# Counting the chosen experts one step later, behind early blocks of the first two experts

## The chip, the cores and the metric

The kernel runs on one NeuronCore of a Trainium2 chip. Its engines are TensorE (PE, with a separate queue for weight loads, PEld), VectorE (DVE), ScalarE (ACT), GpSimd (POOL) and SyncE (SP, which here only issues DMAs). The metric is the device time of one execution in microseconds, as the median of several runs.

## What is computed

Three layers follow each other: causal attention with a decay, a dense feed-forward layer (2304 tokens, 512 wide, 2048 hidden), and a mixture of eight experts in which each token goes to the one expert with the largest gate.

```python
def _moe_ref(x, w_in, w_out):
    h = x @ w_in
    relu6 = np.clip(h + 3.0, 0.0, 6.0)
    g = h * relu6 / 6.0
    return (g @ w_out).astype(np.float32)

def _moe2_ref(x, w_gate, w_output_gate, w1, w2):
    logits = x @ w_gate
    e_idx = np.argmax(logits, axis=1)
    ...
    gate_w = probs[np.arange(N), e_idx]
    eom = 1.0 / (1.0 + np.exp(-(x @ w_output_gate)))
    for e in range(E):
        mask = e_idx == e
        ...
        h = np.maximum(x[mask] @ w1[e], 0.0)
        ye = h @ w2[e]
        out[mask] = gate_w[mask, None] * eom[mask, e, None] * ye
```

## The kernel before

**Numbers.** Every product is made of three matmuls of half-width parts (high times high, high times low, low times high), so each block of weights against a block of tokens costs three instructions. 

**The first two layers** share one long stretch: `moe1_steps` (L683) works on six chunks of 384 tokens, with L695 for the first weight and L718 for the second, and the attention (`attn_seq`, L557) is advanced between its steps. In this stretch a scheduler with a simulated timeline sets the order of every engine but SP, from priorities that follow the order of the code. A chunk of tokens, once it is out of the dense layer, goes through `gate_steps(c)` (L773), a generator: its first part multiplies with the gate weights (36 small matmuls, L783) and sends the rows through a DMA transpose (L791) to DRAM (`rows`, L793); the second part finds the best expert (L797 to L806), keeps a running count of the chosen experts over the 128-token tiles (`ohsum`, L809), multiplies it with a triangular matrix to get each token's rank in its expert (L814, L815), and makes the table entries `M` (L837). For the first five chunks the parts are run between steps 3, 5 and 7 of the next chunk.

**The seam.** After the last chunk nothing of the first two layers is left to interleave. The code there runs all of `gate_steps(5)`, then `count_rounds` (L886, one matmul L889 and the counts per expert, `cnt`). Then the order is written out by hand for PE, ACT and DVE (`manual_schedule`): two blocks of the first expert, `rank_onehot` for the last three tiles (L938), the `table` (L909: matmuls L916 and a chain of small DVE operations that ends in row numbers `ids`), and then the rest of the first products of experts 0 and 1 (`expert1`, L963, eight blocks of twelve matmuls each, L976, with L979 on ACT and L980 on DVE to empty each block's bank). These first products read 128 rows per expert that have been gathered earlier, from the first 15 tiles alone. They are followed by their second products (`expert2`, L984, L995).

**Behind the seam**, `round_` (L1160) gathers the other rows of every expert by index (L950 on POOL, an indirect DMA that needs `ids` and all of `rows`), transposes them (L953, a DMA that SP issues), multiplies them with both weights, and writes results out by index (L1002). The weights of experts 2 to 7 stream in meanwhile (`stw`, L866), and are split by ACT and DVE (L878, L879).

The blocks of the first two experts take their PSUM banks from the pool `ps_mm`, which has three; the pool `ps2` with five is opened only in front of `round_`:

```python
    first = [expert1(e, ps_mm, (0,)) for e in range(2)]
    ...
    ps2 = ctx.enter_context(tc.tile_pool(name="ps2", bufs=5, space=PSUM))
```

Of the kernel before, what the change touches and what calls it, by code (L numbers as in the profile page):

```python
# [15 lines left out]
PSUM = bass.MemoryType.PSUM  # L16
# [42 lines left out]
def attention_moe_kernel(ctx: ExitStack, tc: tile.TileContext, q, k, v, f, w_in, w_out,  # L59
# [5 lines left out]
    E, _, F2 = w1.shape  # L65
# [13 lines left out]
    ps_mm = ctx.enter_context(tc.tile_pool(name="ps_mm", bufs=3, space=PSUM))  # L79
# [693 lines left out]
    def gate_steps(c):  # L773
# [34 lines left out]
        for i in range(n):  # L808
            nc.vector.tensor_tensor(out=ohsum[:, f0 + i + 1], in0=ohsum[:, f0 + i], in1=oh[:, f0 + i],  # L809
                                    op=ALU.add)  # L810
        pr = ps_mm.tile([P, 512], F32, tag="mm", name="mm")
        for i in range(n):
            o = pr[:, i * E:(i + 1) * E]
# [72 lines left out]
    def count_rounds():  # L886

        ps = ps_mm.tile([P, 512], F32, tag="mm", name="mm")
        nc.tensor.matmul(ps[:, 0:E], lhsT=allone, rhs=ohsum[:, NB], start=True, stop=True)  # L889
        mx = mp2.tile([P, 1], F32, tag="cmx", name="cmx")  # L890
        more = mp2.tile([P, 8], F32, tag="more", name="more")
        nc.vector.tensor_reduce(out=mx, in_=ps[:, 0:E], axis=AX.X, op=ALU.max)
        nc.vector.tensor_tensor(out=more, in0=mx.to_broadcast([P, 8]), in1=thr, op=ALU.is_gt)
        nc.vector.tensor_reduce(out=mx, in_=more, axis=AX.X, op=ALU.add)
        nc.vector.tensor_copy(out=nrounds, in_=mx)
        nc.vector.tensor_copy(out=cnt, in_=ps[:, 0:E])
# [12 lines left out]
    def table(R, s0, pool, ps_pool, blocks, nb):  # L909


        n = len(blocks)
        sel = ps_pool.tile([P, 512], F32, tag="mm", name="mm")
        for j, s in enumerate(blocks):
            for i in range(nb):
                nc.tensor.matmul(sel[:, j * NV * E:(j + 1) * NV * E], lhsT=R[:, i, s * P - s0:(s + 1) * P - s0],  # L916
                                 rhs=M[:, i].rearrange("p a e -> p (a e)"), start=i == 0, stop=i == nb - 1)
        T = lambda nm, sh, dt: pool.tile(sh, dt, tag=f"{nm}{n}", name=nm)
        sv = T("sv", [P, n, NV, E], F32)
        nc.vector.tensor_copy(out=sv, in_=sel[:, 0:n * NV * E].rearrange("p (s a e) -> p s a e", a=NV, e=E))  # L920
        ids, u, cf = T("ids", [P, 2, n, E], U32), T("u", [P, n, E], F32), T("cf", [P, n, E], F32)
        nc.vector.scalar_tensor_tensor(out=u, in0=sv[:, :, 0], scalar=float(P), in1=sv[:, :, 1], op0=ALU.mult,
                                       op1=ALU.add)
        nc.vector.tensor_copy(out=ids[:, 0], in_=u)
        nc.vector.tensor_tensor(out=u, in0=u, in1=sv[:, :, 6], op=ALU.add)
        nc.vector.scalar_tensor_tensor(out=u, in0=sv[:, :, 2], scalar=-4096.0, in1=u, op0=ALU.mult, op1=ALU.add)
        nc.vector.tensor_scalar(out=ids[:, 1], in0=u, scalar1=4096.0, scalar2=None, op0=ALU.add)
        nc.vector.tensor_tensor(out=cf, in0=sv[:, :, 3], in1=sv[:, :, 4], op=ALU.add)
        nc.vector.tensor_tensor(out=cf, in0=cf, in1=sv[:, :, 5], op=ALU.add)
        for j, s in enumerate(blocks):  # L930
            slot[s] = (ids[:, 0, j], ids[:, 1, j], cf[:, j])
# [5 lines left out]
    def rank_onehot(R, i, s0, s1):  # L937
        nc.vector.tensor_scalar(out=R[:, i], in0=iota[:, s0:s1], scalar1=rank[:, i:i + 1], scalar2=None,  # L938
                                op0=ALU.is_equal)
# [23 lines left out]
    def expert1(e, ps_pool, blocks):  # L963

        W1, (xs, o) = wts[e, 0], xs_t[e, blocks[0]]
        hT, ho = h_t[e, blocks[0]]
        w = len(blocks) * P
        hs = slice(ho, ho + w)
        for m in range(F2 // P):
            ps = ps_pool.tile([P, 512], F32, tag="mm", name="mm")  # L970
            i = 0
            for j in range(KD):
                for a, b2 in ((0, 0), (0, 1), (1, 0)):
                    l = W1[:, a, j, m * P:(m + 1) * P]
                    r = xs[:, b2 * KD + j, o:o + w]
                    nc.tensor.matmul(ps[:, 0:w], lhsT=l.bitcast(BF16) if a else l, rhs=r.bitcast(BF16) if b2 else r,  # L976
                                     start=i == 0, stop=i == 3 * KD - 1)
                    i += 1
            nc.scalar.activation(out=hT[:, m, 0, hs], in_=ps[:, 0:w], func=AF.Relu)  # L979
            nc.vector.scalar_tensor_tensor(out=hT[:, m, 1, hs].bitcast(BF16), in0=ps[:, 0:w], scalar=0.0,  # L980
                                           in1=hT[:, m, 0, hs], op0=ALU.max, op1=ALU.subtract)
            yield
# [25 lines left out]
    def run(g, n=1):  # L1008

        last = None  # L1010
        for _ in range(n):
            r = next(g, "end")
            last = r or last
            if r == "end":
                break
        return last
# [46 lines left out]
    gq = []  # L1063
# [12 lines left out]
    for c in range(NCH):  # L1076
# [55 lines left out]
        if c < NCH - 1:  # L1132
            while len(complete) < need[c + 1]:
                adv()
        gq.append(gate_steps(c))
    for g_ in gq:
        for _ in g_:
            pass
    run(wg_, 4 * KD + 1 - nw)
    count_rounds()  # L1140
    ET = mybir.EngineType

    first = [expert1(e, ps_mm, (0,)) for e in range(2)]
    manual = ctx.enter_context(ExitStack())
    manual.enter_context(tc.manual_schedule(engines={ET.PE, ET.Activation, ET.DVE}))
    run(first[0], 2)
    for i in range(NBL, NB):
        rank_onehot(R, i, P, CAP)
    table(R, P, const, ps_mm, (1, 2), NB)
    for g_ in first:  # L1150
        run(g_, F2 // P)
# [2 lines left out]
            pass  # L1154
    moe1_ctx.close()
    xp = ctx.enter_context(tc.tile_pool(name="xp", bufs=1))
    ps2 = ctx.enter_context(tc.tile_pool(name="ps2", bufs=5, space=PSUM))
    regs = []

    def round_(first):  # L1160
# [85 lines left out]
```

## Time and profile before

| | us |
|---|---|
| median of 3 runs | 831.59 (827.8 to 831.8) |
| the profiled execution | 830.41 |
| its span, from the first to the last instruction | 828.7 |
| the stretch of attention and dense layer with gates in it | about 190 to 588 |
| the seam | about 588 to 619 |
| the experts' rounds | 619 to the end |

The rows below come from the profiled execution. Times count from its first instruction. "Idle before" is the time for which the engine had nothing to run, with the instruction that ended it behind the arrow.

### The profile page before, as it was taken

The page shows a single profiled execution, that of the slowest core. Times are in us where ns is not written, and L with a number is a line of the kernel's source. Part 1 is how long each engine was busy: PE and PEld are TensorE (multiplying, and loading weights), DVE is VectorE, ACT ScalarE, POOL GpSimd, SP SyncE. Part 2 cuts the span into 40 slices and gives each one's busy share as a digit, 9 for nine tenths or more (in the row PEclk, how much of TensorE's full clock was granted, in tenths as well). Part 3 has the DMA queues.
Part 4 walks back from the last instruction along what each step waited for, and adds up shares of the span by engine and source line. Part 5 has one row for each costly group of instructions (what it writes and reads, how often), then busy time and mean ns, then how long its engine had stood idle before and what let it go on. Part 6 is the DMA issues. An engine that isn't in the chain of part 4 may idle for free.

```text
span 828.7 us, 16710 instructions
## 1 busy us (share of the span) xinstructions
PE 744.0 (90%) x6177; PEld 478.4 (58%) x6177; DVE 470.3 (57%) x1267; ACT 449.9 (54%) x909; POOL 317.2 (38%) x393
## 2 busy tenths in 40 slices
PE   4745989978899999998999999999899999999993
PEld 2533556645655655565665666566668665667641
DVE  7998988547651865158623776760313555554510
ACT  4864789756882775277724654550113545454510
POOL 9546788845753463145522500000131232310010
PEclk9986989989999999998999999999999999999997
DMA  8758799979985783497623847612474899895410
GB/s 248 214 184 192 180 214 257 193 128 167 176 154 116 138 141 74 74 145 143 107 55 67 145 138 238 177 41 51 78 150 94 240 281 267 231 265 200 149 37 29
DMA packets 263778, 127.95 MB, mean 154 GB/s; under 512 B 214658, under 2 KB 247522, under 8 KB 263684
## 3 DMA queue, kind: packets, MB, share of 16 engines
q1 hardware_dynamic: 251860, 105.20, 58.5%
q0 software_dynamic: 4960, 15.73, 5.5%
q10 hardware_dynamic: 6864, 5.80, 2.6%
q8 instruction: 54, 0.88, 0.4%
q14 instruction: 40, 0.33, 0.1%
HBM read 71.52 MB, written 10.08 MB: 98 GB/s over the span
## 4 chain that ended last, share of the span: by engine, by line
PE 38%; DMA 28%; DVE 11%; issue 7%; ACT 7%; POOL 4%; SPq 2%; ACTq 0%; another core or an unknown queue 0%; POOLq 0%; DVEq 0%
PE mm L718 14%; PE mm L695 12%; DMA out_dram<-y,ids 7%; DMA stw<-in_moe_w_dram 4%; DMA xg<-rows,ids 4%; PE mm L976 4%; DMA pt<-pn 3%; PE mm L995 3%; PE sc L295 2%; DMA q<-qp 2%; DMA K<-kp 2%; DVE W L879 1%; ACT ms L376 1%; DMA ldk<-in_k_dram 1%; DVE g L707 1%
## 5 line engine op out<-in xcount | busy, mean ns | idle before, releaser
L695 PE MATMUL mm<-xT,wi 128*128 128x384 f16 (+1 forms) x1152 | 213.3, 335 | 7.5 <-DMA xT<-xn 5.1
L718 PE MATMUL mm<-g,wo 128*128 128x384 f16 (+1 forms) x1152 | 199.8, 326 | 1.9 <-ACT g L703 1.1
L695 PEld LDWEIGHTS <-wi 128*128 128x128 f16 (+1 forms) x1152 | 112.1, 100 | 85.2 <-issue 19.7
L718 PEld LDWEIGHTS <-wo 128*128 128x128 f16 (+1 forms) x1152 | 110.7, 98 | 75.2 <-issue 4.6
L976 PEld LDWEIGHTS <-W 128*128 128x128 f16 (+1 forms) x1344 | 100.6, 99 | 16.2 <-issue 8.0
L879 DVE TENSOR_TENSOR W<-stw,W 128x1024 bf16<-128x1024 f32 x64 | 77.7, 1224 | 52.8 <-ACT W L878 48.8
L376 ACT ACTIVATE ms<-ms,nm 128x512 f32<-128x512 f32 (+4 forms) x144 | 78.8, 576 | 48.5 <-DVE nm L342 27.1
L394 POOL TENSOR_TENSOR pn<-ms,pn 128x384 bf16<-128x384 f32 (+1 forms) x80 | 82.4, 1034 | 57.8 <-ACT pn L393 52.6
L976 PE MATMUL mm<-xs,W 128*128 128x256 f16 (+3 forms) x1152 | 97.1, 246 | 4.7 <-DVE hT L980 2.3
L995 PE MATMUL mm<-W,hT 128*128 128x512 f16 (+1 forms) x432 | 94.4, 379 | 1.0 <-DVE hT L980 0.6
L878 ACT ACTIVATE W<-stw 128x1024 f16<-128x1024 f32 x64 | 66.9, 1054 | 47.7 <-DMA stw<-in_moe_w_dram 45.4
L707 DVE TENSOR_TENSOR g<-hr,g 128x384 bf16<-128x384 f32 x80 | 58.1, 726 | 33.6 <-ACT g L703 33.4
L342 DVE CUSTOM_DVE_ANT_1 ms<-sc,mask 128x128 f32<-128x128 f32 (+3 forms) x128 | 59.2, 486 | 26.1 <-PE sc L295 12.1
L995 PEld LDWEIGHTS <-hT 128*128 128x128 f16 (+1 forms) x432 | 41.9, 98 | 51.3 <-issue 1.9
L702 DVE SCALAR_TENSOR_TENSOR hr<-hr,mm 128x384 f32<-128x384 f32 x96 | 52.7, 549 | 28.1 <-ACT hr L699 27.5
L703 ACT ACTIVATE g<-hr 128x384 f16<-128x384 f32 x96 | 49.4, 515 | 28.0 <-DVE hr L702 27.4
L699 ACT ACTIVATE hr<-mm,bias 128x384 f32<-128x384 f32 x96 | 54.4, 567 | 16.5 <-PE mm L695 14.5
L980 DVE SCALAR_TENSOR_TENSOR hT<-mm,hT 128x128 bf16<-128x128 f32 (+1 forms) x96 | 32.0, 355 | 50.4 <-ACT hT L979 48.1
L428 PE MATMUL pv<-vt,pt 128*128 128x65 f16 x320 | 41.2, 198 | 20.9 <-DVE xs L453 9.4
L1002 POOL DMA_INDIRECT out_dram<-y,ids x18 | 20.7, 1148 | 97.9 <-ACT y L1001 57.2
L295 PE MATMUL sc<-K,q 128*128 128x256 f16 (+3 forms) x192 | 48.7, 296 | 6.4 <-DVE nm L342 4.3
L393 ACT ACTIVATE pn<-ms 128x384 f16<-128x384 f32 (+1 forms) x80 | 44.3, 556 | 13.3 <-DMA pt<-pn 12.9
(189 smaller groups left out, 1113.5 us busy)
## 6 DMA issues: line engine op xcount, KB each, us to landing
stw<-in_moe_w_dram SPq DMA_DIRECT2D x64, 512.0 KB
wo<-in_moe_w_in_dram SPq DMA_DIRECT2D x16, 512.0 KB
raw<-in_moe_w_out_dram ACTq DMA_DIRECT2D x11, 512.0 KB
rows<-rw POOLq DMA_DIRECT2D x15, 256.0 KB, 3.5
ldk<-in_k_dram SPq DMA_DIRECT2D x14, 256.0 KB
ldq<-in_q_dram SPq DMA_DIRECT2D x14, 256.0 KB
ldv<-in_v_dram SPq DMA_DIRECT2D x13, 256.0 KB
g<-in_moe_w_out_dram SPq DMA_DIRECT2D x3, 512.0 KB
```

The source lines that it names most:

```text
L295: nc.tensor.matmul(po, lhsT=lhs[0:rows], rhs=r if n > 1 else r[:, :, 0], start=x == 0, stop=x == 1)
L342: nc.vector.tensor_tensor_reduce(out=pairs(ms[:, off:off + w]), in0=ps[:, 0:w].rearrange("p (c j) -> p c j", c=2), in1=pairs(mask[:, 640 - ...
L376: nc.scalar.activation(out=ms[:, off:off + w], in_=ms[:, off:off + w], func=AF.Exp, scale=-1.0, bias=nm[:, i:i + 1])
L394: nc.gpsimd.tensor_tensor(out=lo.bitcast(BF16), in0=ms[:, 0:N], in1=hi, op=ALU.subtract)
L695: nc.tensor.matmul(ps[:, 0:w], lhsT=l.bitcast(BF16) if a else l, rhs=r.bitcast(BF16) if b2 else r, start=i == 0, stop=i == 3 * KD - 1)
L699: nc.scalar.activation(out=hr, in_=ps[:, 0:w], func=AF.Relu, bias=bias3)
L707: either.tensor_tensor(out=g[:, m, 1, 0:w].bitcast(BF16), in0=hr, in1=g[:, m, 0, 0:w], op=ALU.subtract)
L718: nc.tensor.matmul(ps[:, 0:w], lhsT=l.bitcast(BF16) if a else l, rhs=r.bitcast(BF16) if b2 else r, start=i == 0, stop=i == 3 * NF - 1)
L878: nc.scalar.activation(out=hi, in_=sts[i], func=AF.Copy)
L879: nc.vector.tensor_tensor(out=lo.bitcast(BF16), in0=sts[i], in1=hi, op=ALU.subtract)
L976: nc.tensor.matmul(ps[:, 0:w], lhsT=l.bitcast(BF16) if a else l, rhs=r.bitcast(BF16) if b2 else r, start=i == 0, stop=i == 3 * KD - 1)
L995: nc.tensor.matmul(ps, lhsT=l.bitcast(BF16) if a else l, rhs=r.bitcast(BF16) if b2 else r, start=i == 0, stop=i == 3 * NF2 - 1)
```

## The change

`gate_steps` gets one more `yield`, between the running count `ohsum` and the rank matmuls. At the seam the last chunk's gate is no longer run as a whole: two blocks of expert 0 are issued first, then the gate's first two parts, three more blocks, the gate's rest with `count_rounds` and `rank_onehot`, the last three blocks of expert 0 and the first two of expert 1, then the table, and the other six blocks. `ps2` is opened ahead of this and gives the blocks their banks.

```diff
         for i in range(n):
             nc.vector.tensor_tensor(out=ohsum[:, f0 + i + 1], in0=ohsum[:, f0 + i], in1=oh[:, f0 + i],
                                     op=ALU.add)
+        yield
         pr = ps_mm.tile([P, 512], F32, tag="mm", name="mm")
...
-    for g_ in gq:
-        for _ in g_:
-            pass
     run(wg_, 4 * KD + 1 - nw)
-    count_rounds()
     ET = mybir.EngineType
-
-    first = [expert1(e, ps_mm, (0,)) for e in range(2)]
+    ps2 = ctx.enter_context(tc.tile_pool(name="ps2", bufs=5, space=PSUM))
+
+    first = [expert1(e, ps2, (0,)) for e in range(2)]
     manual = ctx.enter_context(ExitStack())
     manual.enter_context(tc.manual_schedule(engines={ET.PE, ET.Activation, ET.DVE}))
+    last, = gq
     run(first[0], 2)
+    run(last, 2)
+    run(first[0], 3)
+    run(last, 2)
+    count_rounds()
     for i in range(NBL, NB):
         rank_onehot(R, i, P, CAP)
+    run(first[0], 3)
+    run(first[1], 2)
     table(R, P, const, ps_mm, (1, 2), NB)
...
-    ps2 = ctx.enter_context(tc.tile_pool(name="ps2", bufs=5, space=PSUM))
```

The lines from L811 on have a number one higher in the new code.

On PE at the seam, before, the rank matmuls (L814, L815) stand right behind the gate's (L783):

```order
L783 LDWEIGHTS x_7847
L783 MATMUL mm<-wg,x_7847 128x16
L814 LDWEIGHTS tri
L814 MATMUL mm<-oh,tri 128x8
L815 LDWEIGHTS allone
L815 MATMUL mm<-ohsum,allone 128x8
```

On PE at the same place with the change, blocks of expert 0 (L977, before L976) stand ahead of them:

```order
L977 LDWEIGHTS W_7129
L977 MATMUL mm<-wi,W_7129 128x128
L815 LDWEIGHTS tri
L815 MATMUL mm<-oh,tri 128x8
L816 LDWEIGHTS allone
L816 MATMUL mm<-ohsum,allone 128x8
```

In all, PE's order at the seam was 36 gate matmuls, 6 for the rank, 1 for the count, 24 of expert 0, 36 of the table, then 168 of experts 0 and 1; it is now 24 of expert 0, 36 gate, 36 of expert 0, 6 rank, 1 count, 60 of experts 0 and 1, 36 table, 72 of expert 1.

On DVE at the seam, before, the gate's second part (up to L836 and M, L837) is mixed with the count (L894, L895) and has two blocks' emptying (L980) in it; L938 are the last tiles' ranks against a ruler:

```order
L894 TENSOR_REDUCE cmx<-more 128x1
L831 CAST vb<-z 128x3
L895 CAST nrounds<-cmx 128x1
L832 CAST vals<-vb 128x3
L833 TENSOR_TENSOR z<-z,vb 128x3
L980 SCALAR_TENSOR_TENSOR wi<-mm,wi 128x128
L834 CAST vb<-z 128x3
L835 CAST vals<-vb 128x3
L836 TENSOR_TENSOR vals<-z,vb 128x3
L980 SCALAR_TENSOR_TENSOR wi<-mm,wi 128x128
L938 TENSOR_SCALAR R<-iota,rank 128x256 x2
L837 TENSOR_TENSOR M<-vals,oh 128x168
```

On DVE with the change, at the end of that stretch, the count (L893 to L897) and the ruler (L939) stand behind M (L838), and five blocks' emptying (L981) stands between them and the table's chain, which begins with L921:

```order
L837 TENSOR_TENSOR vals<-z,vb 128x3
L838 TENSOR_TENSOR M<-vals,oh 128x168
L893 TENSOR_REDUCE cmx<-mm 128x1
L894 TENSOR_TENSOR more<-cmx,thr 128x8
L895 TENSOR_REDUCE cmx<-more 128x1
L896 CAST nrounds<-cmx 128x1
L897 CAST cnt<-mm 128x8
L939 TENSOR_SCALAR R<-iota,rank 128x256 x3
L981 SCALAR_TENSOR_TENSOR wi<-mm,wi 128x128 x5
L921 COPY sv<-mm 128x112
L923 SCALAR_TENSOR_TENSOR u<-sv 128x16
L925 CAST ids<-u 128x16
```

The count moved from inside the gate's chain to behind it, and the blocks' emptying from inside it to behind the ruler. SP's order of transposes and loads behind the seam stays as it was; on POOL one of seven gathers now stands behind the first write of results instead of ahead of it.

The new `yield` also moves the second half of the gates of the first five chunks, since each call now runs a shorter part (the rest falls to step 7 instead of 5), and with it the scheduler's choices from the first gate on. On DVE near the third gate, before, the gate's operations (L804, L805, L809) follow the attention's L469 at once; L707 is the dense layer's:

```order
L707 TENSOR_TENSOR g<-hr,g 128x384
L469 TENSOR_SCALAR xs<-pv,rl 64x64 x2
L804 TENSOR_REDUCE cm<-t_5169 128x3
L805 TENSOR_TENSOR oh<-t_5169,cm 128x24
L809 TENSOR_TENSOR ohsum<-ohsum,oh 128x8
L816 TENSOR_TENSOR t_5171<-lg,oh 128x24
```

On DVE near the third gate with the change, operations of the attention's scores (L342) have come in between, and L816 is L817:

```order
L707 TENSOR_TENSOR g<-hr,g 128x384
L469 TENSOR_SCALAR xs<-pv,rl 64x64 x2
L804 TENSOR_REDUCE cm<-t_5169 128x3
L805 TENSOR_TENSOR oh<-t_5169,cm 128x24
L342 ISA ms,nm<-sc,mask 128x2x64
L342 ISA nm 128x1
L342 ISA ms,nm<-sc,mask 128x2x128
L342 ISA nm 128x1
L809 TENSOR_TENSOR ohsum<-ohsum,oh 128x8
L817 TENSOR_TENSOR t_5171<-lg,oh 128x24
```

The pair L707 and L469 stayed together; what follows them changed places.

## Rows read from the trace of the kernel before

**Rows 1.** Windows by stage: length, busy us (count) by engine, granted clock, DMA share, GB/s.

```profile
core 0: us, PE busy (x) PEld busy (x) DVE busy (x) ACT busy (x) POOL busy (x), PEclk, DMA share, GB/s
190.00:588.00 398.00, 382.88 (x3071) 236.26 (x3068) 220.38 (x675) 221.59 (x451) 135.35 (x169) 0.99 0.61 121
588.00:619.00 31.00, 26.47 (x324) 19.77 (x322) 10.47 (x59) 5.82 (x20) 8.39 (x10) 0.94 0.71 137
643.00:815.00 172.00, 168.15 (x1202) 108.65 (x1199) 79.26 (x114) 80.06 (x130) 34.21 (x29) 1.00 0.68 203
```

**Rows 2.** Timeline of PE at the seam: start, length, line, count, idle before.

```profile
588.33 0.37 PE L783 MATMUL mm<-wg,x 128*128 128x16 f16 x9
589.08 0.21 PE L783 MATMUL mm<-wg,x 128*128 128x16 f16 x2 [0.37 <-ACT x L727]
589.67 0.79 PE L783 MATMUL mm<-wg,x 128*128 128x16 f16 x25 [0.39 <-DVE x L728]
591.84 0.18 PE L814 MATMUL mm<-oh,tri 128*128 128x8 f16 x1 [1.38 <-DVE oh L805]
...
592.53 2.72 PE L976 MATMUL mm<-wi,W 128*128 128x128 f16 x24
595.04 0.77 PE L916 MATMUL mm<-M,R 128*128 128x56 bf16 x15
596.57 0.86 PE L916 MATMUL mm<-M,R 128*128 128x56 bf16 x21 [0.77 <-DVE M L837]
597.28 5.57 PE L976 MATMUL mm<-wi,W 128*128 128x128 f16 x96
603.07 0.83 PE L976 MATMUL mm<-wi,W 128*128 128x128 f16 x12 [0.22 <-DVE wi L980]
605.26 3.51 PE L976 MATMUL mm<-wi,W 128*128 128x128 f16 x60 [1.36 <-DVE wi L980]
608.61 10.52 PE L995 MATMUL mm<-W,wi 128*128 128x512 f16 x48
618.97 3.51 PE L976 MATMUL mm<-xs,W 128*128 128x128 f16 x60
```

**Rows 3.** Windows of three pieces of the seam, columns as in the first group.

```profile
588.00:592.00 4.00, 1.86 (x43) 1.44 (x41) 1.96 (x12) 0.71 (x2) 0.00 (x0) 1.00 0.74 36
592.00:595.50 3.50, 3.46 (x41) 3.21 (x39) 2.27 (x21) 0.69 (x3) 0.59 (x1) 0.51 0.77 153
595.50:599.00 3.50, 2.73 (x62) 2.61 (x60) 2.44 (x13) 0.53 (x3) 1.11 (x2) 1.00 0.80 260
```

**Rows 4.** Timeline of DVE at the seam.

```profile
590.50 0.21 DVE L797 COPY lg<-mm 128x48 f32<-128x48 f32 x1 [0.88 <-PE mm L783]
...
592.21 0.16 DVE L809 TENSOR_TENSOR ohsum<-ohsum,oh 128x8 f16<-128x8 f16 x1
592.43 0.18 DVE L822 TENSOR_TENSOR t<-mm,oh 128x24 f32<-128x24 f32 x1
...
596.44 0.28 DVE L938 TENSOR_SCALAR R<-iota,rank 128x256 f16<-128x256 f16 x1
...
598.62 0.17 DVE L927 TENSOR_SCALAR ids<-u 128x16 uint32<-128x16 f32 x1
```

**Rows 5.** Timeline of POOL behind the seam.

```profile
600.32 0.99 POOL L950 DMA_INDIRECT xg<-rows,ids  x1 [2.70 <-PE mm L976]
...
609.21 0.94 POOL L950 DMA_INDIRECT xg<-rows,ids  x1 [5.37 <-DMA xs<-xg]
612.36 0.94 POOL L950 DMA_INDIRECT xg<-rows,ids  x1 [2.21 <-DMA xs<-xg]
```

**Rows 6.** Line 1194 on SP's queue, the reading of the counts.

```profile
L1194 SPq TENSOR_LOAD <-cnt x8: 262/388/1098, 594.9 to 600.5; - x8
```

**Rows 7.** PE's longest wait from 190 to 588 us, and line 707 (ns: min/median/max).

```profile
PE pv L428 <- DVE xs L469: 4.7, 1, 4.7
L707 DVE TENSOR_TENSOR g<-hr,g x80: 537/559/4343, 183.4 to 558.5; 128x384 bf16<-128x384 f32 x80
```

## Prediction

> **What bounds the kernel now.** I first read the windows by stage [rows 1]. From 190 to 588 us PE is busy 382.9 of 398 us, and from 643 to 815 us 168.2 of 172: there the time is PE's, and nothing off its path counts. In the 31 us of the seam it is busy only 26.5, at a mean clock of 0.94. So the seam is where this change can earn, and what it earns is read as one number: when PE starts the first matmul on newly gathered rows, 618.97 us [rows 2].
>
> The timeline of PE [rows 2] shows what the 30.64 us from 588.33 to there are made of. The gate's matmuls wait twice (0.37 and 0.39 us) for the last columns of x2 to be emptied by ACT and DVE. Then PE waits 1.38 us for DVE to find the chosen expert. 24 matmuls of expert 0 follow in 2.51 us (592.53 to 595.04), the table waits 0.77 us for M, and the other 168 matmuls take 11.33 us (597.28 to 608.61) with two waits (0.22 and 1.36 us) behind DVE's emptying of banks. A steady run of the same matmuls is the last 60: 605.26 to 608.61, or 0.0558 us each. At that rate the 24 would take 1.34 us; they are slow because the granted clock fell to 0.51 from 592.0 to 595.5 us, after a stretch in which PE was busy 1.86 of 4 us [rows 3].
>
> **The change, part by part.**
>
> *PE's order at the seam.* I lay the same instructions along the new order, each at its rate from [rows 2], from 588.33 us on.
> - 24 of expert 0, which need nothing from x2: 24 x 0.0558 = 1.34, to 589.67. That is when x2's last columns were ready before, so both short waits are covered.
> - 36 gate matmuls: the three pieces were busy 0.37 + 0.21 + 0.79 = 1.37 us, with their overlapping ends counted thrice; 1.2, to 590.9.
> - 36 of expert 0: 2.01, to 592.9. Meanwhile DVE finds the expert. From the copy of the logits to the last running count it needed 590.50 to 592.37 us [rows 4], 1.9 us; its start moves from 590.50 to about 590.9, and fewer operations are mixed in, so the count is there by 592.8 and the 1.38 us wait is covered, just.
> - 7 small matmuls for rank and count: 592.53 - 591.84 = 0.69 before, with waits in it. Bounds 0.2 and 0.7, I take 0.3: 593.2.
> - 60 of experts 0 and 1: 3.35, to 596.5.
> - The table's first 15, which need only old tiles: about 0.5, to 597.0. The other 21 need the ruler. 36 in all.
> - 21 of the table: 597.28 - 596.57 = 0.71. Then 72 of expert 1: 4.02. Then L995, 608.61 to 618.97 = 10.36.
>
> *DVE's chain* decides the gap in front of the 21. The gate's second part (16 operations), the count (5) and the ruler (3) now start when the emptying of block 4 is done, some 0.6 us behind PE's 592.9, at 593.5. From L797 to L822 fourteen operations took 590.50 to 592.43 [rows 4], 0.14 us each; 24 of them are 3.3 us and end at 596.8. If each waits its full length of about 0.2 us for the one before, they take 4.8 and end at 598.3. I take 597.4, nearer to the first since half of them are independent: PE waits 0.4 us, with bounds of 0 and 1.3.
>
> *The banks.* Between the emptying of block 4 and the end of the ruler DVE empties nothing, and exactly five blocks are issued by PE in that time. With the three banks of `ps_mm` PE would stand still for two of the five; with the five of `ps2` it does not. The cost of that edit alone is nothing, and its cover is the number five. The waits of 0.22 and 1.36 us sit behind ACT and DVE at 603 to 605 us. I don't know what held ACT there. With five banks PE can run two blocks, 1.3 us, further ahead, so most of the 1.58 us goes; bounds 0 and 1.6 left, I take 0.4.
>
> *Sum.* 597.0 + 0.4 + 0.71 + 4.02 + 10.36 + 0.4 = 612.9 against 618.97: 6.1 us earlier. The bounds add to 5 us (late ruler, waits stay in part) and 6.7 us (neither).
>
> *Does PE get its rows by 612.9?* The gather of the first rows started at 600.32 us [rows 5]. The fourth gather, at 609.21, had waited for the buffer that the first transpose frees, so the first rows were transposed by then, and the second rows by 612.36. That is ahead of 612.9 and, for the second, of 612.9 + 96 x 0.0558 = 618.3. In the new order `ids` comes later: the ruler at 597.4, then the 21 matmuls, five banks to empty, and the chain, near 599.9 instead of 598.8 [rows 4]. The first gather also needed the last rows in DRAM, which don't move; POOL stood idle until 600.32, 1.5 us after `ids` was done. So it moves by 0 to 1 us, and the slack of 3.7 us (612.9 - 609.2) covers that. SP reads the counts in front of the transposes, 594.9 to about 600.8 [rows 6]; the counts now come about 2 us later, so SP is free at about 603, still ahead of the landing of the gather.
>
> *Behind the seam* everything waits for PE: the transposes for expert 2 need a buffer that expert 0's product frees, and the splitting of its weights stands behind expert 1's blocks on ACT and DVE. From 643 us PE is idle 3.9 of 172 us [rows 1], so there is no store of waiting that would swallow the gain, and the 6.1 us reach the end.
>
> *The long stretch before.* The new `yield` moves the second half of five gates, and the scheduler has reshuffled every engine from about 198 us on. The matmuls are the same, so what can change is waiting: 15.1 us in this stretch [rows 1]. The largest piece is one wait of 4.7 us behind DVE's L469, which stood behind an L707 that took 4.34 us instead of the typical 0.56 [rows 7]. L707 and L469 are neighbours again in the new order. Bounds by this row: one such wait less (-4.7) or one or two more (+4.7, +9.4). Nothing in the rows says which; I take 0.
>
> The profiled execution took 830.41 us, and 830.41 - 6.1 = 824.3. The median of the runs is 1.2 above it, which gives 825.5; I predict 825.0.
>
> **Rivals.**
>
> *The clock falls all the same.* It fell from 1.00 to 0.51 behind a stretch with 1.86 of 4 us busy [rows 3]. In the new order PE has work in that stretch, but 36 of its matmuls are 16 columns wide, and the table waits again. If the same 3.5 us run at half rate, 1.7 us are lost: 612.9 becomes 614.6, and the time 826.7. The granted clock in the windows from 589 to 598 decides. [...]
>
> *The rows come too late.* If the gather starts more than about 3.7 us later (counts, `ids` or SP's reads each late), PE waits for rows instead. At 3 us beyond the slack the gain halves: 827.5. Against it stand the slacks above.
>
> *The stretch before gets better.* If the 4.7 us wait is gone, 825.0 - 4.7 = 820.3. For it: the change moves the very operations around L469. Against it: L707 and L469 still stand together.
>
> *The stretch before gets worse: slower.* The mechanism is an L707 stretched to 4.34 us with attention work behind it on DVE, and PE waiting 4.7 us for that. One more is 829.7, no measurable change; from two on the kernel is slower than the profiled 830.41: 834.4. It happened once among 80 in the old order [rows 7], so two more would be a changed pattern, but five gates are moved. [...]
>
> *The change does nothing at the seam*, since PE waits for the rows whatever it does ahead of them, cannot be: the second rows were ready 6.6 us before PE came for the first.
>
> **How the numbers follow.** Half a per cent (4.2 us) is about what a measurement of this kernel can tell from no change; faster means below 827.4. My chances: seam gain in full with the stretch before within 2 us, 0.45; the clock falls, 0.12; rows late, 0.07; stretch better by about 4.7, 0.16; worse by one such wait, 0.14; by two or more, 0.06. Faster takes in the first, the better stretch and most of the clock case: 0.68. Same takes in the late rows, one more wait and the rest: 0.26. Slower is 0.06. The range goes from below the better stretch, 819, to above one more wait, 831, and leaves out the slower case and the tails of the others. The likeliest case alone would be 823 to 827.
>
> **What the new profile would show.** PE goes from its last L718 to L977 without a gap; rank matmuls start within 0.3 us of the third block's end; the clock is 1.00 from 589 to 598; a gap of at most 1.3 us stands in the table; L996 begins at 602 to 603 us of the old time scale, and the first matmul on gathered rows at 612 to 614. The stretch from 190 to 588 us ends within 2 us of the old time. I am wrong if the last L718 moves by more than 4 us, if PE waits for transposed rows behind L996, or if the later rounds give the gain back in waits for weights.

## The result, and the profile after

The changed kernel took 820.85 us (median of 7 runs, 817.04 to 828.27) against 831.18 of the kernel before in the same runs (7, 827.8 to 831.8): ratio 0.9884, interval 0.9857 to 0.9911. That is 10 us faster, inside the predicted range of 819 to 831 and 4 us below the predicted 825.0. It lies nearer to the 820.3 of the rival with a better stretch, which had set the lower end of that range.

The profiled execution of these runs was the longest of the seven (828.27 us), so I read a second one of the same code beside it, called **again** below (813.19 us, its shortest). The first group shows the windows of the long stretch and of the seam of the first one, columns as in [rows 1]:

```profile
190.00:592.80 402.80, 386.54 (x3151) 239.66 (x3148) 218.61 (x686) 226.26 (x460) 138.79 (x174) 1.00 0.60 121
592.80:617.60 24.80, 23.89 (x321) 17.70 (x320) 10.74 (x59) 6.27 (x21) 6.51 (x8) 1.00 0.58 136
```

The seam now fits into 24.8 us, PE is busy in 23.9 of them, and the clock is 1.00 throughout (0.94 in [rows 1]). PE's timeline of again answers to [rows 2]; start, length, line, count, idle before:

```profile
580.01 1.50 PE L977 MATMUL mm<-wi,W 128*128 128x128 f16 x24
581.35 1.05 PE L783 MATMUL mm<-wg,x 128*128 128x16 f16 x36
582.25 2.17 PE L977 MATMUL mm<-wi,W 128*128 128x128 f16 x36
584.26 0.17 PE L815 MATMUL mm<-oh,tri 128*128 128x8 f16 x1
...
584.44 3.51 PE L977 MATMUL mm<-wi,W 128*128 128x128 f16 x60
587.79 0.55 PE L917 MATMUL mm<-M,R 128*128 128x56 bf16 x15
588.61 1.06 PE L917 MATMUL mm<-M,R 128*128 128x56 bf16 x21 [0.27 <-DVE R L939]
589.50 4.18 PE L977 MATMUL mm<-wi,W 128*128 128x128 f16 x72
593.52 10.52 PE L996 MATMUL mm<-W,wi 128*128 128x512 f16 x47
604.30 3.58 PE L977 MATMUL mm<-xs,W 128*128 128x128 f16 x60 [0.26 <-issue]
608.64 3.57 PE L977 MATMUL mm<-xs,W 128*128 128x128 f16 x61 [0.76 <-DVE hT L981]
```

From the first early block to the first gathered row it is 604.30 - 580.01 = 24.29 us (24.66 in the first profile), where [rows 2] have 30.64. All waits of [rows 2] are gone but one of 0.27 us in the table. A small one at 604.30 is new; the one behind `hT` at 608.64 had 0.52 us in the kernel before. The clock, in windows that answer to [rows 3]:

```profile
579.00:583.00 4.00, 4.00 (x82) 3.58 (x80) 1.54 (x6) 1.04 (x3) 0.00 (x0) 1.00 0.14 30
583.00:586.50 3.50, 3.50 (x70) 3.50 (x68) 3.14 (x21) 1.48 (x7) 0.94 (x2) 1.00 1.00 194
586.50:590.00 3.50, 3.23 (x72) 2.92 (x69) 3.26 (x21) 0.83 (x3) 0.26 (x2) 1.00 0.44 156
```

DVE's chain (answering to [rows 4]), the last write of rows and the first gather on POOL ([rows 5]) and the reading of the counts by three engines ([rows 6]), all of again:

```profile
582.44 0.21 DVE L797 COPY lg<-mm 128x48 f32<-128x48 f32 x1 [0.29 <-PE mm L783]
...
584.98 0.17 DVE L817 TENSOR_TENSOR t<-lg,oh 128x24 f32<-128x24 f32 x1
...
588.20 0.16 DVE L897 CAST cnt<-mm 128x8 int32<-128x8 f32 x1
588.27 0.67 DVE L939 TENSOR_SCALAR R<-iota,rank 128x256 f16<-128x256 f16 x3
...
590.36 0.17 DVE L925 CAST ids<-u 128x16 uint32<-128x16 f32 x1
```

```profile
589.97 0.54 POOL L793 DMA_DIRECT2D rows<-wi  x1 [3.24 <-DMA wi<-x]
593.21 0.99 POOL L951 DMA_INDIRECT xg<-rows,ids  x1 [2.70 <-PE mm L977]
```

```profile
L1198 SPq TENSOR_LOAD <-cnt x8: 262/264/524, 588.4 to 592.9; - x8
...
L1198 PEldq TENSOR_LOAD <-cnt x8: 300/312/927, 600.0 to 604.0; - x8
L1198 ACTq TENSOR_LOAD <-cnt x8: 274/384/708, 604.1 to 607.3; - x8
```

In the long stretch the 4.34 us L707 and the 4.7 us wait of [rows 7] are gone. Line 707 (ns: min/median/max), and PE's longest waits from 353.44 to 436.89 us, the part where the 4.7 us stood (in total, times, longest), again:

```profile
L707 DVE TENSOR_TENSOR g<-hr,g x80: 527/558/1939, 182.4 to 550.2; 128x384 bf16<-128x384 f32 x80
```

```profile
PE mm L695 <- DVE hr L702: 1.7, 1, 1.7
PE mm L815 <- DVE hr L702: 1.2, 1, 1.2
PE mm L718 <- DVE hr L702: 1.1, 1, 1.1
```

### The profile page after: what moved, and what is told of

The parts are those of the page before. It is cut to its first block, busy times and chain, and to the rows that moved or that the text cites. A ratio compares the mean times of both kernels' runs of the same rounds, so it can differ in the third digit from the quotient of the medians.

```text
span 826.5 us, 16712 instructions
## 1 busy us (share of the span) xinstructions
PE 741.9 (90%) x6166; PEld 478.6 (58%) x6177; DVE 466.5 (56%) x1267; ACT 450.2 (54%) x909; POOL 318.0 (38%) x393
## 4 chain that ended last, share of the span: by engine, by line
PE 41%; DMA 28%; DVE 11%; issue 7%; ACT 7%; POOL 4%; SPq 1%; ACTq 0%; POOLq 0%; DVEq 0%
PE mm L718 19%; PE mm L695 10%; DMA out_dram<-y,ids 8%; DMA pt<-pn 5%; DMA xg<-rows,ids 4%; PE mm L977 4%; PE mm L996 2%; DMA stw<-in_moe_w_dram 2%; DMA q<-qp 2%; DMA K<-kp 2%; PE sc L295 2%; DVE ms L342 2%; POOL pn L394 1%; ACT ms L376 1%; DVE cv L658 1%
## 5 line engine op out<-in xcount | busy, mean ns | idle before, releaser
L718 PE MATMUL mm<-g,wo 128*128 128x384 f16 (+1 forms) x1152 | 200.0, 328 | 1.7 <-DVE hr L702 1.7
L718 PEld LDWEIGHTS <-wo 128*128 128x128 f16 (+1 forms) x1152 | 111.5, 98 | 75.9 <-issue 5.4
L977 PEld LDWEIGHTS <-W 128*128 128x128 f16 (+1 forms) x1344 | 99.5, 98 | 15.0 <-issue 7.7
L977 PE MATMUL mm<-xs,W 128*128 128x256 f16 (+3 forms) x1152 | 97.0, 246 | 5.2 <-DVE hT L981 3.0
L996 PE MATMUL mm<-W,hT 128*128 128x512 f16 (+1 forms) x422 | 93.8, 379 | 1.1
L342 DVE CUSTOM_DVE_ANT_1 ms<-sc,mask 128x128 f32<-128x128 f32 (+3 forms) x128 | 59.0, 484 | 27.3 <-PE sc L295 13.5
L707 DVE TENSOR_TENSOR g<-hr,g 128x384 bf16<-128x384 f32 x80 | 54.1, 678 | 33.3 <-ACT g L703 33.1
L996 PEld LDWEIGHTS <-hT 128*128 128x128 f16 (+1 forms) x432 | 41.8, 98 | 51.0 <-issue 1.6
L703 ACT ACTIVATE g<-hr 128x384 f16<-128x384 f32 x96 | 49.3, 516 | 24.1 <-DVE hr L702 23.5
L981 DVE SCALAR_TENSOR_TENSOR hT<-mm,hT 128x128 bf16<-128x128 f32 (+1 forms) x96 | 31.6, 353 | 49.9 <-ACT hT L980 49.4
L428 PE MATMUL pv<-vt,pt 128*128 128x65 f16 x320 | 42.0, 198 | 17.9 <-DVE xs L453 10.8
L728 DVE SCALAR_TENSOR_TENSOR x<-mm,x 128x384 bf16<-128x384 f32 x24 | 13.2, 555 | 71.7 <-ACT x L727 71.7
```

What stands on the lines that cost most here:

```text
L342: nc.vector.tensor_tensor_reduce(out=pairs(ms[:, off:off + w]), in0=ps[:, 0:w].rearrange("p (c j) -> p c j", c=2), in1=pairs(mask[:, 640 - ...
L707: either.tensor_tensor(out=g[:, m, 1, 0:w].bitcast(BF16), in0=hr, in1=g[:, m, 0, 0:w], op=ALU.subtract)
L996: nc.tensor.matmul(ps, lhsT=l.bitcast(BF16) if a else l, rhs=r.bitcast(BF16) if b2 else r, start=i == 0, stop=i == 3 * NF2 - 1)
```

## The experiments

Kernels of one group ran on one chip, beside the kernel before; its own median was 828.38 us in the first group, 825.19 in the second and 827.25 in the third, so ratios are compared across groups, not times. This table holds all that compute the whole result. The three stages add up to the profiled span but for the first 151 to 158 us: the stretch goes from the first to the last L727 (the emptying of x2 on ACT), the seam from PE's first instruction behind the last L718 to its first matmul on gathered rows, and the rest from there to the end. "Order" is that of the long stretch, and "PE idle" is the time between the ends of the stretch in which PE was not busy.

| kernel | order | us (runs) | ratio to before, interval | stretch | PE idle | seam | rest |
|---|---|---|---|---|---|---|---|
| before | old | 831.18 (7) | | 434.7 | 20.3 | 30.64 | 209.7 |
| after | new | 820.85 (7) | 0.9884 (0.9857, 0.9911) | 435.5 | 21.4 | 24.66 | 208.9 |
| again | new | 817.96 (7) | 0.9886 (0.9865, 0.9907) | 427.3 | 14.8 | 24.29 | 207.2 |
| seam_only | old | 822.27 (10) | 0.9939 (0.9918, 0.996) | 434.3 | 20.8 | 24.37 | 207.3 |
| yield_only | new | 823.89 (12) | 0.995 (0.9924, 0.9976) | 432.0 | 16.2 | 30.61 | 208.2 |
| three_banks | new | 820.12 (6) | 0.9901 (0.9881, 0.9922) | 430.8 | 15.0 | 26.33 | 206.8 |
| gate_first | new | 819.33 (9) | 0.9928 (0.9903, 0.9953) | 433.0 | 17.4 | 25.80 | 206.0 |
| table_mid | new | 823.13 (12) | 0.9975 (0.995, 1.0) | 429.4 | 17.9 | 28.47 | 207.0 |
| early_regs | new | 818.9 (12) | 0.9926 (0.99, 0.9951) | 429.1 | 15.4 | 27.95 | 205.2 |
| yield_early | third | 820.56 (12) | 0.9961 (0.9939, 0.9983) | 427.7 | 15.8 | 30.79 | 206.3 |
| control | new | 818.27 (6) | 0.9888 (0.985, 0.9925) | 430.5 | 16.6 | 24.28 | 208.6 |
| mid_regs | new | 818.12 (6) | 0.9892 (0.9859, 0.9926) | 429.2 | 17.8 | 23.87 | 207.4 |
| steps_367 | fourth | 827.54 (12) | 1.0009 (0.9985, 1.0034) | 434.6 | 20.6 | 30.81 | 207.4 |

The seam repeats within 0.4 us where its code is the same. The stretch does not: nine profiles of the new order lie between 427.3 and 435.5, so a single profile can't weigh a change there. PE's idle time sorts them better: 20.3 to 20.8 us in the old and the fourth order, 14.8 to 17.9 in the third and in eight of the nine profiles of the new one. The ninth, after, has 21.4 and was the longest of its seven executions.

### First group: the two halves of the change

**again** is the changed kernel with no edit.

> The changed kernel unchanged, for a second profile beside its runs of 817.0 to 828.3 us (median 820.85, 10.3 below before). If the profiled execution of 828.27 us was an odd one, late by about 4 us before the seam, this profile ends its last L718 near 588 us or earlier and the run near 821; the seam (last L718 to the first matmul on gathered rows, without its wait for issue) is 24 to 25 us long in either.

**seam_only** has the new seam and the old order ahead of it:

```diff
-        yield
+        if c == NCH - 1:
+            yield
```

> The seam's new order alone: the new yield only for the last chunk, so all engines keep the order of before up to the seam. Theory A (seam 6 us, the rest of the 10.3 us gain from the scheduler's new order of the long stretch): 825 us, last L718 where it was before (588 to 589). Theory B (the seam is worth 10 us and the long stretch nothing): 821 us. Theory C, as predicted: seam 6, long stretch 0, the rest noise: 825, but then the run of the whole change comes back near 825 too.

**yield_only** is the kernel before with nothing but the new `yield`, which is run through at once at the old seam:

```diff
                                     op=ALU.add)
+        yield
         pr = ps_mm.tile([P, 512], F32, tag="mm", name="mm")
```

> The new yield alone, with the seam as before: order of the long stretch as in the changed kernel. Theory A: 827 us (4 below before). Theories B and C: 831, as before.

**three_banks** takes the early blocks' banks from the pool of three:

```diff
-    first = [expert1(e, ps2, (0,)) for e in range(2)]
+    first = [expert1(e, ps_mm, (0,)) for e in range(2)]
```

> The whole change, but the blocks of experts 0 and 1 take their banks from ps_mm (three) instead of ps2 (five). If the fifth bank is what covers DVE's long chain, PE stands still for two of the five blocks and the seam grows by 1.3 to 3 us against the changed kernel's: 822 to 824. If the blocks wait for nothing there, it is the same within 0.5 us.

Against the kernel before, the median of seam_only is 6.1 us lower (822.27 against 828.38), that of yield_only 4.5 and that of the whole change 10.4. By the ratios it is 5.0 (3.3 to 6.8), 4.1 (2.0 to 6.3) and 9.4 us (7.7 to 11.2). Either way the halves add up, and what the seam's own length says, 30.64 - 24.3 = 6.3, lies inside its interval. Theory A holds; the reshuffle of the long stretch, which I had taken as nothing, is a real gain of about 4 us.

In three_banks PE's timeline shows where the missing banks cost:

```profile
592.88 1.50 PE L977 MATMUL mm<-wi,W 128*128 128x128 f16 x24
596.17 2.29 PE L977 MATMUL mm<-wi,W 128*128 128x128 f16 x36 [1.79 <-DVE cnt L897]
```

Of the five blocks between the rank matmuls and the table PE issues two and then stands 1.79 us. What ends the wait is `cnt` (L897), DVE's last reading of the count's bank, and not the emptying of a block: in this kernel the rank and the count take their banks from the same three. The seam is 2.0 us longer than again's; the median is 2.2 us higher, and by the ratios it is 1.2, within their intervals.

### Second group: the terms of the seam, and another order

**gate_first** gives up the cover of the two short waits:

```diff
-    run(first[0], 2)
-    run(last, 2)
+    run(last)
+    run(first[0], 2)
+    run(last)
     run(first[0], 3)
```

> The gate's 36 matmuls go ahead of the first two early blocks again; all else is the changed kernel. Theory: the 24 matmuls cover the two short waits for x2 (0.37 and 0.39 us), and no more: the seam, 24.3 us in the changed kernel, becomes 25.1, the time 0.8 us longer than the changed kernel's 818. Rival: those 24 matmuls also keep the clock up; if the gate with its two waits comes first, the granted clock falls to about 0.5 for some 3.5 us as it did before the change, which costs 1.7 us more: seam 26.8, time 820.5.

The seam is 1.5 us longer than again's, not 0.8. PE's timeline:

```profile
586.34 0.21 PE L783 MATMUL mm<-wg,x 128*128 128x16 f16 x2 [0.37 <-ACT x L727]
586.93 0.79 PE L783 MATMUL mm<-wg,x 128*128 128x16 f16 x25 [0.38 <-DVE x L728]
...
590.96 0.18 PE L815 MATMUL mm<-oh,tri 128*128 128x8 f16 x1
...
591.59 3.51 PE L977 MATMUL mm<-wi,W 128*128 128x128 f16 x60
```

Both waits are back, and the seven small matmuls take 0.63 us (590.96 to 591.59) where again has 0.18. The rival did not come: in the window from 586 to 590 us, with PE busy 3.27 of 4 us, and in the two behind it, the clock was 1.00.

**table_mid** moves the table between the second products:

```diff
-    table(R, P, const, ps_mm, (1, 2), NB)
...
         for _ in expert2(e, None, ps_mm, (0,), wi[:, 1, e, 0:2 * DM].bitcast(F32)):
             pass
+        if e == 0:
+            table(R, P, const, ps_mm, (1, 2), NB)
```

> The table and its chain stand between the second products of experts 0 and 1 instead of ahead of expert 1's last six blocks, so the row numbers are done about 9.5 us later (591.2 becomes 600.7 on the scale of the changed kernel's second profile) and the first gather, which started at 593.2, starts at about 600.9, 7.7 us later. Theory of the prediction: PE has a slack of 3.7 us before it waits for gathered rows, so it stands still for about 4 us behind its second L996 and the time is 4 us longer, 822. Rival one: the rows were ready far earlier than PE took them (the slack is 7 us or more), nothing is lost: 818. Rival two: PE was already waiting for rows (no slack): 7.7 us lost, 825.7, no faster than the old seam by more than 3 us.

PE's and POOL's timelines:

```profile
599.72 5.34 PE L996 MATMUL mm<-W,wi 128*128 128x512 f16 x24
608.87 3.33 PE L977 MATMUL mm<-xs,W 128*128 128x128 f16 x31 [3.81 <-DMA xs<-xg]
```

```profile
601.38 1.01 POOL L951 DMA_INDIRECT xg<-rows,ids  x1 [0.41 <-issue]
```

The first gather starts 601.38 - 580.40 = 20.98 us into the seam instead of 593.21 - 580.01 = 13.20, that is 7.8 later, and the seam grows by 28.47 - 24.29 = 4.2. So the changed kernel has 3.6 us to spare for its rows. The ratio is 0.9 per cent above the changed kernel's, some 7 us and more than these 4.2; the profiled execution was the shortest of the twelve, and what made the others longer no profile shows.

**early_regs** reads the counts ahead of the second products:

```diff
+    regs = [nc.values_load(cnt[0:1, e:e + 1], min_val=0, max_val=NT) for e in range(E)]
     for e in range(2):
         for _ in expert2(e, None, ps_mm, (0,), wi[:, 1, e, 0:2 * DM].bitcast(F32)):
...
-        if first:
-            regs.extend(nc.values_load(cnt[0:1, e:e + 1], min_val=0, max_val=NT) for e in range(E))
```

> The reading of the eight counts into registers stands ahead of the second products of experts 0 and 1 instead of behind them, for every engine. Theory: of what is left of the seam, 0.26 us in front of the first gathered matmuls (TensorE reads counts there) and 0.76 us a little later (ScalarE reads counts from 604 to 607 and empties the first bank too late) come from these readings; both go, and the time is 1.0 us shorter than the changed kernel: 817. Rival: TensorE's own reading then stands where it has no lead, in front of the first L996, and the 0.3 us are paid there, so that 0.5 to 0.7 us are won or nothing: 817.5 to 818.

Worse than the rival: PE stood 2.23 us in front of L996, and the clock fell behind that. PE's timeline, and the window behind the wait:

```profile
597.27 12.21 PE L996 MATMUL mm<-W,wi 128*128 128x512 f16 x48 [2.23 <-issue]
```

```profile
597.20:609.30 12.10, 12.03 (x48) 5.10 (x48) 0.00 (x0) 0.69 (x1) 4.80 (x5) 0.86 0.84 181
```

L996 took 12.21 us instead of 10.52, 1.7 more at a mean clock of 0.86. The seam lost 3.7 us; the two small waits behind it went, and the rest is 2.0 us shorter than again's, which is within what it varies by among the profiles (205.2 to 209.7).

By their ratios gate_first and early_regs are 3 us slower than the changed kernel, with 2 us of uncertainty on each; the lengths of the seam are the sharper measure here.

**yield_early** is the kernel before with a yield at another place of the gate:

```diff
         nc.vector.tensor_copy(out=lg, in_=ps[:, 0:n * 16].rearrange("p (n e) -> p n e", e=16))
+        yield
         mx, cm = sm("mx", 1), sm("cm", 1)
```

> The kernel before, with its old seam, and an extra yield at another place of the gate: right behind the copy of the logits, so that nearly all of the gate's second half moves to the next chunk's step 7. It deals the scheduler's order in the long stretch anew, in a third way. Theory one: the old order was unlucky (the 4.34 us L707 with a 4.7 us wait of TensorE behind it) and nearly any other order is better: 3 to 5 us faster than before, and no L707 above 2.1 us. Theory two: the place of the yield behind the count is what helps, or each order is a draw of its own: within 2 us of before or slower, with long waits at other places.

The median is 4.6 us below before's, by the ratio 3.2 us (1.4 to 5.0), with no L707 above 1.59 us: within the intervals this order is as good as the new one.

### Third group: a fourth order, the counts once more, and the long L707 by itself

**control** is the changed kernel.

> The changed kernel with no edit, beside the two that follow on the same chip. Expected 1.1 per cent below the kernel before, as in its first two timings; seam 24.3 to 24.7 us, no L707 above 2.1 us.

It came out so: 1.1 per cent, a seam of 24.28 us, and no L707 above 1.94 us.

**mid_regs** has the same `regs` line as early_regs, but behind the second product of expert 0 (`if e == 0`).

> The eight counts are read into registers between the second products of experts 0 and 1. Theory: what made the earlier place cost 4 us was that TensorE's queue had run ahead only by short instructions there; behind 24 matmuls of 512 columns its lead is over 4 us again, so nothing is paid on TensorE, and ScalarE has the counts before it has to empty the first bank of gathered rows: the wait of 0.76 us behind DVE hT goes, and the 0.26 us in front of the gathered rows too. Seam 24.0 to 24.3, time 0.8 to 1.0 us below the changed kernel. Rival: TensorE stands still for 2 us or more in the middle of L996 as it did in front of it; then it is 1 to 3 us slower than the changed kernel.

The 0.26 us in front of the gathered rows are gone and the seam is 0.4 us shorter, but the time is that of control within their intervals: 818.12 and 818.27. A wait for `hT` of 0.66 us is left, and PE waits 0.46 us between the first blocks. A gain of this size can't be told from none here.

**steps_367** is the kernel before with another step for the gates' second half:

```diff
-            if gq and k_ in (3, 5, 7):
+            if gq and k_ in (3, 6, 7):
```

> The kernel before with no yield added; of the first five gates the second half runs at step 6 of the next chunk instead of step 5. A fourth order of the long stretch, made without the change's edit. Theory one (the old order was unlucky): the 4.34 us L707 and the 4.7 us wait are gone, and the time is 3 to 5 us below the kernel before. Theory two (each order is a draw of its own, or the rank's move to step 7 is what helps): within 2 us of the kernel before, or slower.

No change (1.0009), though the wait of 4.7 us is gone here too (the longest L707 is 3.29 us). So "nearly any other order is better" falls: of three orders other than the old one, two gain 3 to 4.5 us and one nothing.

**port** starts DVE operations beside rows of POOL operations:

```python
    def trial(n, x):
        nc.vector.tensor_tensor(out=trig, in0=a, in1=lo[3], op=ALU.subtract)
        for i in range(n):
            nc.gpsimd.tensor_tensor(out=lo[i], in0=trig, in1=h, op=ALU.subtract)
        for _ in range(5):
            nc.vector.tensor_scalar(out=small, in0=small, scalar1=1.0, scalar2=None, op0=ALU.add)
        x()
```

> No part of the kernel's work: DVE operations alone and beside a row of POOL operations, all in SBUF, to see what makes an L707 long. A DVE subtraction of two SBUF operands, 128x384, is started shortly after the first of 0, 1, 2 or 4 POOL subtractions (128x512, about 1.16 us each) that stand back to back. Theory: it ends only when the whole row on POOL has ended: about 0.56, 1.2, 2.4 and 4.7 us long. An operation with one SBUF operand, and one with a PSUM and an SBUF operand, keep about their own length (0.3 to 0.6 us) beside four of POOL's. Rival: DVE gets in between two of POOL's operations, so that none is longer than one POOL operation and its own length, 1.7 us; or they share, and all are about twice their own length; then the 4.34 us have another cause.

It missed what it was made for. Its timeline on DVE and POOL, with no POOL operation and with four:

```profile
3.11 0.98 DVE L86 TENSOR_SCALAR small<-small 128x8 f32<-128x8 f32 x5
4.00 0.55 DVE L90 TENSOR_TENSOR res<-a,h 128x384 bf16<-128x384 f32 x1
...
11.85 4.67 DVE L86 TENSOR_SCALAR small<-small 128x8 f32<-128x8 f32 x5
12.01 4.48 POOL L84 TENSOR_TENSOR lo<-trig,h 128x512 bf16<-128x512 f32 x4 [1.58 <-DVE small L86]
16.43 0.55 DVE L99 TENSOR_TENSOR res<-a,h 128x384 bf16<-128x384 f32 x1
```

The five small operations that were only to fill time took 4.67 us instead of 0.98, and the subtraction began at the end of POOL's row (16.43 us, the row's end 16.49). But they show something: of these five, one took 0.16 us and the other four 1.07 to 1.14 each, one beside each of POOL's four operations of 1.15. What made them so long no run here shows.

## Why the prediction was right, and where it was short

**The seam, term by term.** From the start of the seam, in us, forecast against again: 24 early matmuls 1.34 and 1.34; the gate 1.2 and 0.90; 36 matmuls 2.01 and 2.01; seven small ones 0.3 and 0.18; 60 matmuls 3.35 and 3.35; the table with its wait 1.61 and 1.71 (the wait 0.4 and 0.27); 72 matmuls 4.02 and 4.02; the stall left behind DVE and ACT 0.4 and 0; L996 10.36 and 10.78. Forecast 24.6, measured 24.3 to 24.7, and 5 to 6 us won in time (seam_only, 3.3 to 6.8): this step was right in its parts too. Two sums beside it are off without bearing on this: the upper bound of the gain is 6.1 + 0.4 + 0.4 = 6.9 and not 6.7, and the prediction gives no reason for 825.0 where its sum gives 825.5. The last term holds a cost that I had not seen. 0.26 us of it are TensorE's own reading of the counts, which runs from 600.0 to past 604.0 behind L996.

**The banks.** "PE would stand still for two of the five" with three banks came out as 1.79 us of waiting behind the second block and 2.0 us of seam. The size was right. The reason was so only in part: of the three banks the rank and the count hold two, and PE went on when DVE had read the count, 0.45 us before DVE began to empty a block.

**The rows in time.** I gave a slack of 3.7 us, table_mid shows 3.6. The first gather starts 13.2 us into the seam instead of 600.32 - 588.33 = 12.0, 1.2 later where I allowed 0 to 1. My reason for the little shift, that the last rows in DRAM "don't move", was wrong. In the kernel before, the last write of rows was

```profile
597.08 0.54 POOL L793 DMA_DIRECT2D rows<-wi  x1 [0.60 <-DMA wi<-x]
```

that is 8.75 us into the seam; in again it starts at 589.97, 9.96 us into it and 1.2 later, behind a transpose. In both the gather follows 3.24 us after this write, so it moved with the rows and not with `ids`. PE's first gathered matmul waits for the reading of counts, not for rows.

**The clock rival** fell: 1.00 in all windows of the seam, and even in gate_first, where PE waits twice. What holds it was not tried further; in [rows 3] it fell to 0.51 behind a stretch with 1.86 of 4 us busy.

**Behind the seam** nothing gave the gain back: the rest is 205 to 209 us in every profile with a changed seam and 206 to 210 in those with the old one.

**The stretch before was the step that was mis-sized.** I wrote "Nothing in the rows says which; I take 0". It is worth about 4 us (yield_only, 0.9924 to 0.9976). The prediction's own sign, "I am wrong if the last L718 moves by more than 4 us", came out in both profiles: the seam begins at 592.97 us in the first and at 580.01 in again, where it was 588.33. My rival had the size, 4.7, but only in part the reason. It counted the one wait of 4.7 us as the loss.

Over the whole stretch the gain is idle time. Windows of it in before, then in yield_only, which has the old seam and the new order:

```profile
153.85:588.50 434.65, 414.34 (x3383) 255.68 (x3382) 236.51 (x731) 244.68 (x502) 156.99 (x199) 0.98 0.63 124
```

```profile
151.77:583.75 431.98, 415.75 (x3384) 256.69 (x3382) 234.15 (x731) 245.19 (x502) 156.88 (x199) 0.98 0.62 124
```

PE idles 20.3 us in the first and 16.2 in the second, 4.1 less. It is busy 1.4 us longer in the second, and the mean clock is the same, so in this pair the clock does not make the gain. Most of the difference is made in the part from the first chunk's end to the second's, with the first gate: PE idles 12.7 us there in before, 12.2 in seam_only, 12.1 in steps_367, and 8.7 to 10.4 in again, control, yield_only, mid_regs and yield_early. A wait of 1.7 to 2.0 us for DVE's L368 stands in before, seam_only and steps_367 and not in again, and one of 1.1 us behind ACT's L703 in before and not in steps_367 or again; the rest is in smaller pieces. Why the new order waits less there stays open.

The part with the 4.7 us shows less of that, and here the clock bears on the time. In the old order the part with that wait is 88.7 us long (356.80 to 445.50) and PE idles 5.0 of them; in again it is 83.45 and PE idles 4.2. So the wait was mostly replaced, by those of 1.7, 1.2 and 1.1 us shown above. What went there is mainly the slow clock behind it. Windows of seam_only (old order), then of again, at that place:

```profile
371.00:376.00 5.00, 0.53 (x7) 0.28 (x5) 4.76 (x3) 2.76 (x9) 4.11 (x5) 0.94 0.73 147
376.00:382.00 6.00, 5.61 (x29) 2.98 (x30) 5.70 (x30) 5.90 (x14) 2.45 (x4) 0.50 0.93 183
```

```profile
369.00:376.00 7.00, 4.11 (x48) 2.88 (x46) 6.58 (x27) 4.60 (x12) 3.87 (x6) 1.00 0.99 188
376.00:382.00 6.00, 5.81 (x51) 3.76 (x49) 5.45 (x22) 5.95 (x14) 2.07 (x2) 1.00 1.04 149
```

Behind the one long wait of seam_only the clock stood at 0.50 for 6 us, which is worth 3 us of full speed; behind the shorter waits of the new order it stayed at 1.00 in again, and fell to 0.58 for 4 us in control, whose part is 85.38 us long. Of the nine profiles of the new order five fall there (a mean clock of 0.91 to 0.92 from 370 to 390 us) and four do not (1.00). That is one way in which runs of one order differ. steps_367 has a shorter part here (82.35 us) but not the shorter first one, and loses 3.8 us in the part between (91.60 against 87.76) and 2.1 in the last.

**What made L707 long** is only argued. In seam_only it stands over a row of five POOL operations without a gap, DVE's row first:

```profile
371.22 4.32 DVE L707 TENSOR_TENSOR g<-hr,g 128x384 bf16<-128x384 f32 x1 [2.71 <-ACT g L703]
```

```profile
370.76 1.17 POOL L215 TENSOR_TENSOR kp<-ldk,kp 64x512 f16<-64x512 f32 x1
371.87 0.92 POOL L394 TENSOR_TENSOR pn<-ms,pn 128x384 bf16<-128x384 f32 x1
372.74 1.13 POOL L318 TENSOR_TENSOR vt<-ldv,vt 128x512 bf16<-128x512 f32 x1
373.82 0.43 POOL L457 TENSOR_TENSOR xn<-xs,xn 128x128 bf16<-128x128 f32 x1
374.21 0.90 POOL L394 TENSOR_TENSOR pn<-ms,pn 128x384 bf16<-128x384 f32 x1
```

It ends at 375.54, 0.43 us behind the row's end at 375.11. The same remainder stands in steps_367 (L707 of 3.29 us, 0.43 behind a row that ends at 284.89) and in again (1.94 us, 0.42 behind one that ends at 210.49). So L707 seems to wait out a whole row, where port's small operations each took about as long as one POOL operation (1.07 to 1.14 us beside 1.15). No POOL instruction in this row is longer than 1.17 us, so the length of a single one does not explain the 4.32 us. Why the two differ no run shows, and what in the order of the code makes such meetings stays open too.

## What to carry to other kernels

Lay the same instructions along the new order with rates from a steady run, count the banks between two emptyings, and check what must arrive by then: at the seam that gave each term to a few tenths. Price a long wait of TensorE with the slow clock behind it: 4.7 us of waiting cost 3 us more (6 us at 0.50 in seam_only), and shorter waits in its place saved some or all of that (4 us at 0.58 in control, 1.00 in again). But don't take the longest wait for the loss of a stretch: add up the idle time of the whole of it, which was 4 us shorter in yield_only, most of it at another place. And where an edit moves a scheduler's order, test that half alone: it was about 4 of the 10 us here, another order gave nothing, and profiles of one order differ by 8 us, so only timings weigh it.

## What I had not expected of the hardware

TensorE's reading of eight counts took 3 to 4 us (600.0 to past 604.0 in again, 593.9 to about 597.2 in early_regs). Behind matmuls of 512 columns (again) all but 0.26 us of it was hidden, since the reading started 4.3 us ahead of the matmul that stands next; behind matmuls of 128 columns (early_regs) it started 1.1 us ahead of the end of PE's work, and PE stood still for 2.23 us. And in port a DVE operation of 128x8 elements, 0.16 us ahead of POOL's row, took 1.07 to 1.14 us beside it.
